# Another issue order for the backward chain of a memory-augmented attention kernel

## The chip, the cores and the metric

The kernel runs on one core of a Trainium2 chip. The metric is the device time of one execution in microseconds (us); the time before is the median of three runs, 2872.61 us (2855.53 to 2875.89). The engines are TensorE (PE; its weight loads are shown as PEld), VectorE (DVE), ScalarE (ACT), GpSimd (POOL) and SyncE (SP), which issues DMAs. GpSimd issues DMAs too.

## The reference

The reference computes a forward pass and all its gradients. The forward is a residual sum of two branches over the same normalised rows: an attention branch that walks over 64 segments of 32 rows and carries 8 memory rows from one segment to the next, and a dense branch with a squared relu.

```python
def _A_ref(x, mem0, Wq, Wk, Wv, Wo, seg_len):
    ...
    for s in range(n_seg):
        xs = x[:, s * seg_len:(s + 1) * seg_len, :].copy()
        h = jnp.concatenate([mem, xs], axis=1)
        q = jnp.einsum('btd,dhe->bhte', h, Wq)
        k = jnp.einsum('btd,dhe->bhte', h, Wk)
        v = jnp.einsum('btd,dhe->bhte', h, Wv)
        scores = jnp.einsum('bhqe,bhke->bhqk', q, k) * scale
        scores = jnp.where(mask[None, None], scores, -1000000000.0)
        p = _softmax(scores, axis=-1)
        o = jnp.einsum('bhqk,bhke->bhqe', p, v)
        o = jnp.einsum('bhte,hed->btd', o, Wo)
        mem = o[:, :M, :].copy()
        outs.append(o[:, M:, :])
    return jnp.concatenate(outs, axis=1)
...
    xn = _layernorm(x, axis=-1)
    return x + _A_ref(xn, A_mem0, A_Wq, A_Wk, A_Wv, A_Wo, A_seg_len) + _B_ref(xn, B_w1, B_b1, B_w2, B_b2)
...
_out, _vjp = jax.vjp(_f, A_x, A_mem0, A_Wq, A_Wk, A_Wv, A_Wo, B_w1, B_b1, B_w2, B_b2)
_grads = _vjp(grad_out)
```

There are 2048 rows of 512, 32 heads of 128. In the backward pass the gradient of a segment's memory rows is what the segment before it needs, so the 64 segments are a chain, walked from the last to the first.

## The kernel before

The kernel runs in stages: the dense branch, the forward chain, a stage for the left parts' softmax gradients with the dense weights' gradients beside it, the backward chain (from 1348.5 us of the profiled span to about 2310), and the large weight gradients at the end. This change is in the backward chain alone.

A *step* of the chain is one segment; four steps are a *block*. I number the steps in the order in which the chain walks them, so that steps 20 to 23 are the first to fourth step of one block. A step has some 60 small operations, each a function that issues a handful of instructions, and an operation has a name:

- o0mm, o1mm (L374): the incoming gradient times Wo, 16 matmuls each; o0ev, o1ev copy the result to SBUF (gON); o0fl, o1fl (L167) transpose it and o0te, o1te copy that (gOT);
- vp0, vp1 (L1389, L1391): products with the probabilities, PD, which pb (L1337) builds on GpSimd out of the loaded P; vea, veb, vla, vlb copy them out into gv and gvL;
- s0, s1 (L464): products with the values, vT, which vc (L1351, L1352) builds on GpSimd out of vl, loaded by vtr (L1346, a transposing DMA); d10 to d41 and tu0, tu1 are the softmax gradient on VectorE;
- kp0, kp1 and qp0, qp1 (L623): gradients of keys and queries, 32 small matmuls each; kea0 to keb1, kla0 to klb1, qea0 to qeb1 copy them out of PSUM into gk, gkL and gq, on ScalarE (L419) or VectorE (L422);
- vg0 to qg1 (L492): "gathers", gv, gk and gq times the weights, 16 matmuls each, summed in ps_gR; the sixth is done in two halves;
- ra, rb, ta, tb, Ha, Hb, xa, xb: the sum R is copied, transposed (L528) and added over head groups; Ha and Hb write the memory rows' gradient into GT, from which the next step's o0mm starts.

An operation that begins with L. is one of the block's "left" part, done once a block for the block before or beside it: L.G0 to L.I3 (L1256) are 12 groups of 8 matmuls, L.ta, L.tb their transposes, L.Vo, L.Ko, L.Qo (L1243) the stores of the block's gv, gk, gq (the tile G4, one buffer) to DRAM, L.sx (L1291) the store of XT, L.ldv and L.ldk loads for the next block. ldp, ldq, ldn (L1332, L1339, L1340) load the next step's P, qN and kN on GpSimd's queue.

The order is written out by hand, in B_ORDER: four strings, one for each step of a block. The number of plus signs behind a name says by how many rounds or steps it is shifted, so that a string may hold operations of several steps. Each engine, and each engine's DMA queue, runs its operations strictly in that order. ENGS says which copies run on ScalarE and which on VectorE.

TensorE's matmuls come in three tile forms, as the profile's rows show them: 128*32 (o0mm, s0, the gathers, L.G to L.I), 32*128 (kp, qp) and 128*128 (o0fl, vp, the transposes). TensorE's order in the four steps of a block, before:

```
1: o0mm o1mm o0fl vp0 L.G2 s0 o1fl vp1 L.I1 L.G1 s1 kp0 vg1 qp0 vg0 kg0 qp1 qg0 kp1 qg1 kg1 L.H2 ta tb
2: o0mm o1mm o0fl vp0 s0 o1fl vp1 L.H1 s1 vg0 kp0 qp0 vg1 qg0 kp1 kg0 qp1 L.I2 kg1 qg1 L.G3 ta tb
3: o0mm o1mm o0fl vp0 s0 o1fl vp1 vg0 s1 kp0 vg1 qp0 L.I3 kg0 kp1 qp1 qg0 kg1 qg1 L.H3 ta tb
4: o0mm o1mm o0fl vp0 o1fl s0 vp1 s1 vg0 L.G0 kp0 L.tb qp0 vg1 kg0 kp1 qp1 L.ta qg0 kg1 qg1 L.I0 ta tb L.H0
```

Of the kernel before, what the change touches and what calls it, by code (L numbers as in the profile page):

```python
# [26 lines left out]
def kernel(  # L27
# [673 lines left out]
    with psum("fr", 4) as fr, psum("fpp", 1) as fpp, \  # L701
# [259 lines left out]
        with tc.manual_schedule():  # L961
# [25 lines left out]
            for n in range(-1, NB + 4):  # L987
                play(F_ORDER, n, steps, lefts, lambda s: s, lambda b: b, done)
# [5 lines left out]
    with sb("la", 2) as la, sb("ls", 2) as ls, sb("lo", 1) as lo_, sb("wg", 2) as wg, psum("lpp", 1) as lpp, psum("lr", 4) as lr:  # L994
# [170 lines left out]
        "pb+++ rb+++ ldq+++ L.H2+ ta+++ tb+++ vc+++ Ha+++ Hb+++ o0mm++++ o0ev++++ o1mm++++ o1ev++++ xb+++ o0fl++++ "  # L1165
# [20 lines left out]
    with sb("bq", 1) as bq, sb("bt", 1) as bt, sb("bs", 2) as bs, sb("be", 1) as be, psum("bpp", 1) as bpp, psum("br", 4) as br:  # L1186
# [274 lines left out]
        with tc.manual_schedule():  # L1461
# [225 lines left out]
```

## Time and profile before

| | us |
|---|---|
| three runs | 2855.53, 2872.61, 2875.89 |
| span of the profiled execution | 2875.6 |
| backward chain, first to last step's start | 1348.5 to 2281.2 |
| TensorE busy in it | 849.3 |
| steps 20, 21, 22, 23 | 16.55, 13.05, 13.45, 15.45 |

The profile gives no time of its own beside the span; the slowest of the three runs is 0.3 us above it. In a row of instructions stand the line, engine, operation, what it writes <- what it reads, the tile form and sizes, the count, the busy time and the mean of one in ns, and then the idle time before them with what ended it. In a table of windows each column is an engine's busy time with the count of its instructions, then the granted TensorE clock, the share of time in which the DMA engines were busy, and GB/s. "Issue" is waiting that the profile explains by no semaphore.

### The profile page before, as it was taken

The numbers are of one execution on the slowest core, as the hardware profiler recorded it, in microseconds if no ns is written. First come the engines' busy times: TensorE is split into PE (matmuls) and PEld (weight loads), VectorE is DVE, ScalarE is ACT, GpSimd is POOL, SyncE is SP. The second block draws the span as 40 slices with busy tenths as digits, with TensorE's granted clock in tenths as the row PEclk, the third lists the DMA queues.
The fourth block names the chain that finished last, engine by engine and source line by source line (L and its number), as shares of the span: only waits on it lengthen the run. The fifth ranks groups of instructions, "written<-read, shape, count | busy, mean of one in ns | idle before, by whom it ended". The sixth has DMA issues, their size and how long they took to land.

```text
span 2875.6 us, 116922 instructions
## 1 busy us (share of the span) xinstructions
PE 2672.8 (93%) x52315; PEld 1447.4 (50%) x52405; DVE 1277.0 (44%) x3755; ACT 1001.7 (35%) x2330; POOL 665.8 (23%) x1289
## 2 busy tenths in 40 slices
PE   7998999999999997788898989999999899999999
PEld 3444555555555555355444544554445444444444
DVE  4534656666666655343444544554445401100000
ACT  2324544444444445232333333333334311111111
POOL 1000000000000000223333433343333434322221
PEclk9999999999999999899999999999999999999999
DMA  9865689899999888987577876788777899999993
GB/s 248 268 204 172 157 201 222 204 215 225 211 208 226 205 210 186 283 243 205 140 172 168 192 210 168 171 195 213 175 168 183 224 294 271 216 211 209 211 207 69
DMA packets 839066, 586.77 MB, mean 204 GB/s; under 512 B 638001, under 2 KB 727618, under 8 KB 835234
## 3 DMA queue, kind: packets, MB, share of 16 engines
q1 hardware_dynamic: 796034, 450.52, 69.2%
q0 software_dynamic: 42384, 128.63, 15.2%
q8 instruction: 411, 6.73, 1.0%
q14 instruction: 93, 0.76, 0.1%
q10 hardware_dynamic: 144, 0.13, 0.0%
HBM read 184.95 MB, written 248.79 MB: 151 GB/s over the span
## 4 chain that ended last, share of the span: by engine, by line
PE 84%; DMA 6%; issue 4%; DVE 4%; ACT 1%; SPq 1%; POOL 0%; ACTq 0%; DVEq 0%; POOLq 0%
PE ps_gw L1645 19%; PE ps_proj L374 16%; PE ps_gR L492 11%; PE ps_R L492 5%; PE ps_tr L167 3%; PE ps_L L374 3%; PE b_pp L623 3%; PE ps_RL L1256 2%; PE ps_sc L464 2%; PE f_pp L623 2%; PE ps_w L1106 2%; PE ps_h L310 2%; PE ps_B L345 2%; PE ps_gxb L354 2%; PE ps_ga L317 2%
## 5 line engine op out<-in xcount | busy, mean ns | idle before, releaser
L1645 PE MATMUL ps_gw<-gn,HNc 128*128 128x512 bf16 x1884 | 414.6, 379 | 1.9
L1645 PEld LDWEIGHTS <-HNc 128*128 128x128 bf16 x1920 | 187.9, 98 | 223.8
L419 ACT CAST f_N<-ps_proj 128x512 bf16<-128x512 f32 x320 | 184.0, 581 | 196.0 <-PE ps_proj L374 189.3
L1579 ACT CAST wt<-ps_gw 128x512 bf16<-128x512 f32 x128 | 73.5, 589 | 437.8 <-PE ps_gw L1645 404.9
L374 PEld LDWEIGHTS <-X 128*32 128x32 bf16 x5760 | 144.8, 96 | 136.0 <-DVE X L537 20.2
L884 POOL COPY kM<-f_kT 128x256 bf16<-128x256 bf16 x64 | 25.8, 403 | 756.3 <-DVE f_kT L422 571.6
L1562 DVE TENSOR_TENSOR gx<-ps_rows,gb 128x512 f32<-128x512 f32 x16 | 11.1, 692 | 402.1 <-PE ps_rows L1560 402.1
L492 PE MATMUL ps_gR<-Wv,gv 128*32 128x512 bf16 x2048 | 143.0, 397 | 8.3 <-issue 8.3
L492 PE MATMUL ps_gR<-Wk,gk 128*32 128x512 bf16 (+1 forms) x2048 | 141.6, 386 | 4.2 <-issue 3.6
L492 PE MATMUL ps_R<-Wo,OT 128*32 128x256 bf16 x4096 | 131.8, 279 | 11.9 <-issue 6.3
L1645 PE MATMUL ps_gw<-GOc,gn 128*128 128x512 bf16 x626 | 138.4, 379 | 2.0 <-DMA GOc<-in_grad_out_dram 1.3
L492 PE MATMUL ps_gR<-Wq,gq 128*32 128x512 bf16 (+1 forms) x2048 | 127.1, 359 | 8.0 <-issue 7.9
L419 ACT CAST gON<-ps_proj 128x512 bf16<-128x512 f32 x128 | 75.0, 586 | 160.2 <-PE ps_proj L374 160.2
L374 PE MATMUL ps_proj<-Wq,X 128*32 128x512 bf16 x1920 | 127.3, 380 | 1.9 <-issue 1.9
L374 PE MATMUL ps_proj<-Wo,GT 128*32 128x512 bf16 x2048 | 123.8, 384 | 5.4 <-DVE GT L1301 5.0
L1580 POOL DMA_DIRECT2D out_dram<-wt x120 | 65.0, 544 | 262.0 <-ACT wt L1579 239.8
L374 PE MATMUL ps_proj<-Wk,X 128*32 128x512 bf16 x1920 | 124.6, 382 | 1.0 <-issue 0.2
L374 PE MATMUL ps_proj<-Wv,X 128*32 128x512 bf16 x1920 | 121.9, 378 | 0.0
L419 ACT CAST gk<-b_pp 128x256 bf16<-128x256 f32 x192 | 69.2, 379 | 146.4 <-PE b_pp L623 104.8
L1332 POOL DMA_DIRECT2D b_P<-S_A x63 | 33.9, 538 | 369.2 <-issue 128.4
L1337 POOL COPY PD<-b_P 32x320 bf16<-32x320 bf16 x256 | 115.6, 451 | 8.9 <-DMA b_P<-S_A 0.3
L492 PEld LDWEIGHTS <-OT 128*32 128x32 bf16 x4096 | 105.7, 98 | 21.0 <-issue 14.1
(291 smaller groups left out, 5280.6 us busy)
## 6 DMA issues: line engine op xcount, KB each, us to landing
S_A<-f_N SPq DMA_DIRECT2D x64, 512.0 KB
out_dram<-wt POOLq DMA_DIRECT2D x134, 128.0 KB, 5.4
S_A<-f_N SPq DMA_DIRECT2D x64, 256.0 KB
S_GB<-gv SPq DMA_DIRECT2D x32, 512.0 KB
S_GB<-gk SPq DMA_DIRECT2D x32, 512.0 KB
S_GB<-gq SPq DMA_DIRECT2D x32, 512.0 KB
b_kN<-S_A POOLq DMA_DIRECT2D x63, 256.0 KB, 4.4
b_qN<-S_A POOLq DMA_DIRECT2D x63, 256.0 KB, 4.3
```

Source lines behind the costliest of these rows:

```text
L167: nc.tensor.transpose(ps_ap, in_ap, ident[base:base + k, base:base + k])
L310: nc.tensor.matmul(ps[:], lhsT=W1[:, dc, fc * P:(fc + 1) * P], rhs=HT[:, dc, :], start=(dc == 0), stop=(dc == DC - 1))
L317: nc.tensor.matmul(ps2[:], lhsT=W2T[:, dc, fc * P:(fc + 1) * P], rhs=gT[:, dc, :], start=(dc == 0), stop=(dc == DC - 1))
L345: nc.tensor.matmul(psB[:], lhsT=aT[:, fc, rc * P:(rc + 1) * P], rhs=W2[:, fc, :], start=(fc == 0), stop=(fc == FC - 1))
L374: nc.tensor.matmul(o, lhsT=hT[:, dc, :], rhs=x, start=(dc == 0), stop=(dc == DC - 1), tile_position=(0, 32 * g))
L419: nc.scalar.copy(out, in_)
L492: nc.tensor.matmul(R[32 * g:32 * g + 32, 0:(cs.stop - cs.start) * P].rearrange("p (a b) -> p a b", b=P), lhsT=XT(k, g), rhs=x[:, cs, :], s ...
L623: nc.tensor.matmul(o, lhsT=N_[32 * g:32 * g + m, kk * P:(kk + 1) * P], rhs=X(kk)[32 * g:32 * g + m], start=(i == 0), stop=(i == len(jobs) ...
L1337: nc.gpsimd.tensor_copy(PD[32 * g:32 * g + 32, g], C["P"][32 * g:32 * g + 32, :, KW - L:KW])
L1579: nc.scalar.copy(wt[:], ps[:])
L1580: eng(dst, wt[:])
L1645: nc.tensor.matmul(ps[:], lhsT=l(rc), rhs=r(rc), start=(n == 0), stop=(n == RC_ALL - 1))
```

## The change

B_ORDER is written anew, with the same operations. Its four strings are cut at another place (a string begins in the middle of one step and ends in the middle of the next), which is why the loops begin at -2. Three copies of a step go from ScalarE to VectorE (kea0, kla1, qea1) and two from VectorE to ScalarE (klb0, qeb1). TensorE's order in the four steps of a block, after:

```
1: o0mm o1mm L.H0 o0fl vp0 o1fl s0 vp1 s1 L.I1 L.G1 vg1 kp0 qp0 vg0 kg0 kp1 qp1 qg0 qg1 kg1 L.H2 ta tb
2: o0mm o1mm o0fl vp0 s0 L.H1 vp1 o1fl vg0 s1 kp0 qp0 vg1 L.I2 qg0 kp1 qp1 kg0 kg1 qg1 ta tb
3: o0mm o1mm o0fl vp0 o1fl s0 vp1 L.G3 L.I3 s1 kp0 qp0 vg0 vg1 kg0 qp1 kp1 qg0 kg1 qg1 L.H3 ta tb
4: o0mm o1mm o0fl vp0 s0 vp1 o1fl L.ta L.tb s1 vg0 kp0 qp0 vg1 kg0 kp1 qp1 L.G0 qg0 L.I0 kg1 qg1 L.G2 ta tb
```

The loads and stores move too. Where a fourth step meets the next first one, SyncE's queue was L.Vo0 L.Vo1 L.qtr L.Ko0 L.lq L.Ko1 L.qst ldk0 ldk1 L.Qo0 | L.Qo1 L.sx vtr, and is L.qtr L.ldt L.lq L.qst L.Vo1 | L.Ko0 L.Vo0 L.Qo1 ldk0 L.Qo0 ldk1 L.sx L.Ko1 vtr (the bar is the step's start in the written order). GpSimd's queue was vc L.ldv L.ldk | pb ldn ldp ldq ldp ldn pb ldq vc, and is L.ldv pb L.ldk ldq vc | ldn ldp ldq ldp ldn vc pb.

```diff
--- before.py
+++ after.py
@@ -984,7 +984,7 @@
                     for i in range(m):
                         ps = fr.tile([P, 8 * P], BF16, name="ps_wt", tag="r")
                         turn_weight(ps, *q.pop(0), acp if k in ("L.S1", "L.ex0", "L.ex1") else (acp, vcp)[i % 2])
-            for n in range(-1, NB + 4):
+            for n in range(-2, NB + 4):
                 play(F_ORDER, n, steps, lefts, lambda s: s, lambda b: b, done)
     sm_cm.__exit__(None, None, None)
     assert not TURNS_O
@@ -1156,33 +1156,37 @@
 
 
     B_ORDER = (
-        "L.vo0+ o0mm++++ o1mm++++ L.vo1+ L.Qo1+ o0ev++++ pb+++ xa+++ L.xt o1ev++++ o0fl++++ xb+++ L.ra0+ vp0++++ "
-        "o0te++++ L.G2+ vea++++ s0++++ d10++++ o1fl++++ d20++++ L.ko0+ d30++++ vla++++ o1te++++ vp1++++ "
-        "ldn+++ L.I1+ L.G1+ d40++++ ldp++++ ldq+++ veb++++ s1++++ d11++++ vlb++++ kp0++++ ldp+++++ vg1++++ L.qo0+ "
-        "tu0++++ L.qo1+ keb0++++ d21++++ qp0++++ kla0++++ L.sx+ vg0++++ kea0++++ d31++++ qeb0++++ d41++++ vtr++++ "
-        "L.ko1+ kg0++++ klb0++++ tu1++++ qp1++++ ldn++++ qeb1++++ qea0++++ qg0++++ qea1++++ kp1++++ qg1++++ keb1++++ "
-        "kea1++++ kg1++++ klb1++++ kla1++++ ra++++",
-        "pb+++ rb+++ ldq+++ L.H2+ ta+++ tb+++ vc+++ Ha+++ Hb+++ o0mm++++ o0ev++++ o1mm++++ o1ev++++ xb+++ o0fl++++ "
-        "vp0++++ xa+++ o0te++++ vla++++ s0++++ o1fl++++ vp1++++ d10++++ vea++++ vtr++++ d20++++ L.H1+ o1te++++ L.ktr+ "
-        "d30++++ d40++++ veb++++ vlb++++ tu0++++ vtr+++++ s1++++ d11++++ d21++++ ldp+++++ d31++++ vg0++++ kp0++++ "
-        "qp0++++ d41++++ vg1++++ qea0++++ qeb0++++ qg0++++ keb0++++ L.kst+ tu1++++ kla0++++ klb0++++ kp1++++ kea0++++ "
-        "kea1++++ kg0++++ qp1++++ keb1++++ kla1++++ qeb1++++ L.ra1+ L.I2+ kg1++++ qea1++++ L.ra2+ qg1++++ klb1++++ "
-        "ra++++ L.G3+ rb++++ ta++++ Ha++++",
-        "vc+++ tb+++ Hb+++ ldq+++ o0mm++++ xb+++ o1mm++++ o0ev++++ o0fl++++ pb+++ xa+++ o1ev++++ o0te++++ vp0++++ "
-        "s0++++ d10++++ vea++++ d20++++ o1fl++++ L.vtr+ vp1++++ o1te++++ vg0++++ vla++++ s1++++ d30++++ d40++++ "
-        "d11++++ L.sl ldn+++ veb++++ tu0++++ d21++++ vlb++++ kp0++++ keb0++++ vg1++++ d31++++ d41++++ L.vst+ L.gs+ "
-        "kea0++++ qp0++++ tu1++++ qea0++++ klb0++++ kla0++++ L.I3+ kg0++++ qeb0++++ kp1++++ L.gl++ qp1++++ ldp+++++ "
-        "qea1++++ kea1++++ keb1++++ qeb1++++ qg0++++ klb1++++ kla1++++ L.gst+ kg1++++ ldq++++ qg1++++ ra++++ L.H3+ "
-        "ta++++ rb++++ Ha++++ tb++++ Hb++++",
-        "o0mm++++ o1mm++++ o0ev++++ vc+++ L.ra3+ ldn+++ xb+++ vtr++++ o1ev++++ xa+++ L.ldt++ o0fl++++ pb+++ vp0++++ "
-        "vc++++ o1fl++++ o0te++++ s0++++ vea++++ vla++++ o1te++++ d10++++ d20++++ vp1++++ s1++++ d30++++ veb++++ "
-        "vlb++++ d40++++ d11++++ vg0++++ L.G0++ kp0++++ L.Vo0++ L.Vo1++ L.tb+ kla0++++ tu0++++ d21++++ qp0++++ vg1++++ d31++++ keb0++++ "
-        "d41++++ kea0++++ kg0++++ kp1++++ L.qtr+ qeb0++++ tu1++++ klb0++++ qp1++++ L.ldv++ L.ta+ qea0++++ "
-        "qg0++++ qeb1++++ kea1++++ L.Ko0++ keb1++++ qea1++++ kg1++++ L.lq++ klb1++++ qg1++++ L.I0++ ra++++ L.ldk++ L.Ko1++ rb++++ "
-        "ta++++ L.qst+ ldk0++++ ldk1++++ L.Qo0++ kla1++++ tb++++ L.H0++ Ha++++ Hb++++")
+        "d20+++++ d30+++++ vg0+++++ d40+++++ vla+++++ o1te+++++ tu0+++++ s1+++++ vtr++++++ kp0+++++ veb+++++ "
+        "vlb+++++ qp0+++++ d11+++++ d21+++++ vg1+++++ qeb0+++++ L.I2+ d31+++++ qea0+++++ qg0+++++ d41+++++ tu1+++++ "
+        "kp1+++++ keb0+++++ qp1+++++ vc+++++ kea0+++++ kla0+++++ kea1+++++ qea1+++++ klb0+++++ keb1+++++ pb+++++ "
+        "L.ko1+ kg0+++++ ldq+++++ L.vo0+ ldn+++++ qeb1+++++ kg1+++++ qg1+++++ L.vtr+ klb1+++++ ra+++++ vc++++++ "
+        "kla1+++++ rb+++++ ta+++++ L.gst+ L.vst+ Ha+++++ tb+++++ L.ko0+ Hb+++++ o0mm++++++ xa+++++ L.gl++ xb+++++ "
+        "o1mm++++++ o0ev++++++ o0fl++++++ o1ev++++++ vp0++++++ vtr+++++++ o1fl++++++ L.ra1+ o0te++++++ s0++++++ "
+        "vp1++++++ o1te++++++ vla++++++ d10++++++ d20++++++",
+        "d30+++++ d40+++++ tu0+++++ L.G3+ L.I3+ s1+++++ kp0+++++ qp0+++++ d11+++++ vea+++++ d21+++++ vg0+++++ "
+        "vlb+++++ d31+++++ veb+++++ vg1+++++ kea0+++++ d41+++++ klb0+++++ L.sl tu1+++++ keb0+++++ kg0+++++ L.vo1+ "
+        "qp1+++++ L.qtr+ qea0+++++ ldp++++++ kp1+++++ kea1+++++ qeb0+++++ qea1+++++ pb+++++ kla0+++++ keb1+++++ "
+        "qg0+++++ qeb1+++++ L.ra2+ kla1+++++ kg1+++++ qg1+++++ ra+++++ klb1+++++ L.H3+ ta+++++ rb+++++ tb+++++ "
+        "Ha+++++ Hb+++++ xb+++++ o0mm++++++ L.ra3+ o1mm++++++ o0ev++++++ o0fl++++++ vp0++++++ o1ev++++++ xa+++++ "
+        "vea++++++ o0te++++++ s0++++++ L.ldt++ vp1++++++ d10++++++ o1fl++++++ L.ta+ L.tb+ d20++++++ vla++++++ "
+        "ldq+++++ o1te++++++ d30++++++ ldn+++++ s1++++++",
+        "d40+++++ tu0+++++ vg0+++++ veb+++++ L.lq++ vlb+++++ kp0+++++ qp0+++++ d11+++++ d21+++++ d31+++++ L.ldv++ "
+        "vg1+++++ kea0+++++ keb0+++++ pb+++++ kg0+++++ d41+++++ kp1+++++ tu1+++++ qeb0+++++ qea0+++++ klb0+++++ "
+        "L.qst+ qp1+++++ kla0+++++ kla1+++++ L.ldk++ kea1+++++ keb1+++++ qeb1+++++ L.G0++ L.xt+ qg0+++++ L.I0++ "
+        "kg1+++++ L.Vo1++ klb1+++++ qea1+++++ qg1+++++ L.G2++ ra+++++ rb+++++ ta+++++ tb+++++ Ha+++++ ldq+++++ "
+        "Hb+++++ vc+++++ o0mm++++++ o0ev++++++ o1mm++++++ L.H0++ ldn+++++ L.Ko0++ L.Vo0++ xa+++++ o0fl++++++ "
+        "o1ev++++++ vp0++++++ o0te++++++ L.qo1++ xb+++++ L.Qo1++ ldk0+++++ o1fl++++++ ldp+++++++ s0++++++ vp1++++++ "
+        "o1te++++++ L.Qo0++ d10++++++ d20++++++ s1++++++",
+        "L.ra0++ ldk1++++ L.sx++ d30+++++ d40+++++ tu0+++++ L.Ko1++ vla+++++ L.I1++ veb+++++ d11+++++ L.G1++ "
+        "vg1+++++ L.qo0 kp0+++++ vlb+++++ qp0+++++ d21+++++ vea+++++ ldq+++++ keb0+++++ kea0+++++ vtr+++++ d31+++++ "
+        "vg0+++++ d41+++++ qeb0+++++ kg0+++++ vtr++++++ L.ktr++ kla0+++++ tu1+++++ klb0+++++ kp1+++++ qp1+++++ "
+        "qea1+++++ ldp+++++ qea0+++++ qeb1+++++ qg0+++++ keb1+++++ ldn+++++ qg1+++++ klb1+++++ kea1+++++ vc+++++ "
+        "kg1+++++ ra+++++ L.H2++ kla1+++++ ta+++++ rb+++++ tb+++++ L.gs++ Ha+++++ L.kst++ Hb+++++ xb+++++ xa+++++ "
+        "pb+++++ o0mm++++++ o0ev++++++ o1mm++++++ o0fl++++++ vp0++++++ o0te++++++ o1ev++++++ vea++++++ s0++++++ "
+        "ldp+++++++ d10++++++ L.H1++ vp1++++++ o1fl++++++")
     ENGS = on_engines(
-        "L.ra0 kea0 keb0 keb1 kla0 kla1 o0ev o1ev qea0 qea1 qeb0 ra vea veb vla vlb",
-        "kea1 klb0 klb1 o0te o1te qeb1")
+        "L.ra0 keb0 keb1 kla0 klb0 o0ev o1ev qea0 qeb0 qeb1 ra vea veb vla vlb",
+        "kea0 kea1 kla1 klb1 o0te o1te qea1")
     with sb("bq", 1) as bq, sb("bt", 1) as bt, sb("bs", 2) as bs, sb("be", 1) as be, psum("bpp", 1) as bpp, psum("br", 4) as br:
         G4 = {n: bq.tile([P, HG, KH, SPB, SEG], BF16, name="g" + n) for n in "vkq"}
         gS = bq.tile([P, KH, KW], BF16, name="gS")
@@ -1484,7 +1488,7 @@
                     steps[NSEG - s][n] = steps[NSEG - 1 - s][n]
             for n in ("vtr", "vc", "ldp", "pb", "ldq", "ldn", "ldk0", "ldk1"):
                 steps[0][n] = lambda: None
-            for n in range(-1, NB + 4):
+            for n in range(-2, NB + 4):
                 play(B_ORDER, n, steps, lefts, lambda s: NSEG - 1 - s, lambda b: NB - 1 - b)
 
             ps = big("ps_m0")
```

## The prediction

> **What bounds the kernel now.** I read the page first, for the busy shares and the chain that ended last.
>
> ```profile
> span 2875.6 us, 116922 instructions
> ...
> PE 2672.8 (93%) x52315; PEld 1447.4 (50%) x52405; DVE 1277.0 (44%) x3755; ACT 1001.7 (35%) x2330; POOL 665.8 (23%) x1289
> ...
> q8 instruction: 411, 6.73, 1.0%
> ...
> PE 84%; DMA 6%; issue 4%; DVE 4%; ACT 1%; SPq 1%; POOL 0%; ACTq 0%; DVEq 0%; POOLq 0%
> ```
>
> TensorE carries 84% of the chain, so what TensorE does not have to do, or does not have to wait for, comes off the end. Next the windows: the whole backward chain, then four successive steps of one block of it (steps 20 to 23, called first to fourth below), then two stretches that I use later.
>
> ```profile
> core 0: us, PE busy (x) PEld busy (x) DVE busy (x) ACT busy (x) POOL busy (x), PEclk, DMA share, GB/s
> 1709.00:1721.27 12.27, 10.26 (x253) 5.99 (x254) 5.67 (x20) 4.15 (x10) 2.73 (x6) 1.00 1.15 377
> ...
> 1761.34:1767.47 6.13, 3.27 (x127) 1.74 (x127) 1.00 (x4) 1.41 (x5) 4.17 (x10) 1.00 1.19 164
> ...
> 1348.50:2281.20 932.70, 849.30 (x22416) 463.05 (x22416) 453.68 (x1420) 354.60 (x960) 357.57 (x694) 0.97 0.74 180
> 1654.00:1670.55 16.55, 13.61 (x368) 7.14 (x356) 6.87 (x25) 6.12 (x16) 4.87 (x10) 1.00 0.94 269
> 1670.55:1683.60 13.05, 12.90 (x356) 7.24 (x356) 7.89 (x23) 5.35 (x15) 4.68 (x9) 1.00 0.53 119
> 1683.60:1697.05 13.45, 12.52 (x349) 6.94 (x348) 6.33 (x21) 5.63 (x15) 2.45 (x5) 1.00 0.43 110
> 1697.05:1712.50 15.45, 14.01 (x361) 7.79 (x364) 8.26 (x24) 5.50 (x15) 10.66 (x22) 1.00 0.99 239
> ```
>
> The chain's 932.7 us hold 849.3 us of busy TensorE: 83.4 us of waiting. The middle steps take 13.05 and 13.45 us, the first 16.55 and the fourth 15.45, and those two are the ones with a DMA share near 1. Then the waits of TensorE within the chain say for whom it waited.
>
> ```profile
> PE b_pp L623 <- issue: 28.5, 23, 3.2
> PE ps_gR L492 <- issue: 19.8, 17, 3.8
> PE b_pp L623 <- DMA b_qN<-S_A: 8.5, 4, 3.8
> PE ps_proj L374 <- DVE GT L1301: 5.0, 1, 5.0
> PE ps_sum L545 <- issue: 4.0, 1, 4.0
> PE b_pp L623 <- DMA b_qNL<-S_NL: 2.9, 1, 2.9
> ```
>
> Three rows of "issue" make 28.5 + 19.8 + 4.0 = 52.3 us, most of the 83.4. "Issue" is a wait that no semaphore explains. I read it as late instructions: queue q8 moved 6.73 MB in 411 packets, and 6.73 MB over 52315 + 52405 instructions of TensorE is 64 bytes each, so a packet holds about 255 of them. Two stretches that I cut from the end of one issue wait to the end of a later one hold 253 + 254 = 507 and 127 + 127 = 254 matmuls and weight loads: two packets and one. TensorE stops where a packet ends, when DMA is busy (shares 1.15 and 1.19).
>
> **The change part by part.** *Fewer changes of tiling.* I sort TensorE's operations by the tile form in their rows (128*32, 32*128, 128*128) and count the neighbours of different form in the two written orders: 51 in a block of four steps before, 40 after (14, 12, 12, 13 against 10 each); over the chain, edges included, 814 and 641. The price is in start-to-start times:
>
> ```profile
> 1675.96 0.20 PE L623 MATMUL b_pp<-gS,b_qN 32*128 32x40 bf16 x4
> ...
> 1676.17 0.21 PE L623 MATMUL b_pp<-gST,b_kN 32*128 32x32 bf16 x4
> ...
> 1676.55 1.05 PE L492 MATMUL ps_gR<-Wv,gv 128*32 128x512 bf16 x16
> 1677.42 1.04 PE L492 MATMUL ps_gR<-Wq,gq 128*32 128x512 bf16 x16
> 1678.39 0.20 PE L623 MATMUL b_pp<-gS,b_qN 32*128 32x40 bf16 x4
> ```
>
> ```profile
> 1660.29 0.20 PE L623 MATMUL b_pp<-gS,b_qN 32*128 32x40 bf16 x4 [1.35 <-DVE ds_t L579]
> ...
> 1660.58 1.05 PE L492 MATMUL ps_gR<-Wv,gv 128*32 128x512 bf16 x16
> ```
>
> A kp followed by a qp of its own form takes 1676.17 - 1675.96 = 0.21 us, one followed by a gather 1660.58 - 1660.29 = 0.29. A gather followed by a gather takes 1677.42 - 1676.55 = 0.87, one followed by a kp 1678.39 - 1677.42 = 0.97. So a change costs 0.08 to 0.10 us, and 173 fewer are worth 173 x 0.09 = **-15.6 us** (13.8 to 17.3), all on TensorE. The Trainium skill ("TensorEngine Tiling (Array Packing)", Key Properties) says that a change of tiling mode drains the engine, and its page "TensorE: Matmul & The Clock Gate" (Step-by-step: what each phase is for) puts the drain near 128 cycles of a 2.4 GHz clock, which as an estimate is 0.053 us, or 9 us for 173. The rows show more, and I take the rows.
>
> *Loads moved.* Behind the two L.ldk loads of the fourth step the old GpSimd queue has pb (four PD copies), then the loads of kN and P, then that of qN for the first step; the new one has pb ahead of L.ldk and qN right behind it. In the old first step qN can land as late as kp0 needs it. The new place gives it the four copies (0.451 us each, row below) and two issues more. I take most of the 8.5 us of waits for b_qN: **-8** (0 to -11.4, with b_qNL).
>
> *Stores moved.* The next rows are the chain in the first step, and SyncE's issues just before.
>
> ```profile
> 1655.07 8.45 DMA S_GB<-gq
> 1663.59 0.38 ACT gq L419
> 1664.22 0.36 DVE gST L482
> 1664.72 0.37 PE b_pp L623 x32
> ```
>
> ```profile
> 1652.64 0.54 SPq L1243 DMA_DIRECT2D S_GB<-gk  x1
> ...
> 1655.07 1.79 SPq L1243 DMA_DIRECT2D S_GB<-gq  x2
> 1656.95 1.26 SPq L1291 DMA_DIRECT2D S_XG<-b_XT  x1
> 1658.46 4.04 SPq L1346 DMA_TRANSPOSE b_vl<-S_A  x1
> ```
>
> ```profile
> 1664.72 0.20 PE L623 MATMUL b_pp<-gST,b_kN 32*128 32x32 bf16 x4 [0.55 <-DVE gST L482]
> ```
>
> G4 has one buffer, so the first copy into gq waits until the store of the last block's gq has read it, 8.45 us after issue; behind it VectorE's transpose, and behind that qp1, 0.55 us late. The new queue puts both gq stores ahead of L.sx and of the second gk store (L.Ko1), and I reckon them out some 3 us earlier: **-8** for 16 blocks x 0.5 (0 to -16). The price is that L.Ko1 comes last, behind L.sx, which waits for xb of the next step: out about 4.5 us into the step instead of 1.4 before its start (1652.64 against 1654.00). With 8.45 us to read, keb1 and kea1 may write at 13, where the stall-free order wants them at about 9 (the starts above, added up to kp1 and qp1) and a step of 16.55 at 12 or later.
>
> *Also in that step*, GpSimd does vc (1.041 + 0.413) before pb (4 x 0.451 = 1.8), where it did pb first:
>
> ```profile
> L1337 POOL COPY PD<-b_P 32x320 bf16<-32x320 bf16 x256 | 115.6, 451 | 8.9 <-DMA b_P<-S_A 0.3
> L1351 POOL COPY b_vT<-b_vl 128x1024 bf16<-128x1024 bf16 x64 | 66.6, 1041 | 70.9 <-DMA b_vl<-S_A 40.0 <-PE ps_sc L464 29.5
> ...
> L1352 POOL COPY b_vT<-b_vTL 128x256 bf16<-128x256 bf16 x64 | 26.4, 413 | 4.2 <-DMA b_vTL<-S_NL 4.1
> ```
>
> The vl transpose goes out behind L.Ko1, at about 5.5; landing like the store before it, 8.5 later, at 14. Then vc to 15.5, pb to 17.3, and vp0 of the next step, 2.1 us into it, needs that pb: the first step cannot be under 15.2 us. It took 16.55 here, so this holds a further gain back rather than adding. For both together I take **+5** (0.3 a block; 0 to 3.5 a block is 0 to +56, the rival below).
>
> *Instruction packets.* kp and qp are 32 matmuls and 32 weight loads in 0.21 to 0.30 us, by far the densest work. Old first step, kp0 to kp1: 4 x 64 + 4 x 32 = 384 instructions in 0.29+0.98+0.30+0.87+0.97+0.30+0.97+0.29 = 4.97 us, 3.3 us a packet. New: kp0 qp0 vg0 kg0 kp1 qp1, 4 x 64 + 2 x 32 = 320 in 0.21+0.30+0.87+0.97+0.21+0.30 = 2.86 us, 2.3 us a packet. A packet in time for 3.3 us can be 1 us late for 2.3; there is one such stretch in each of the two DMA-heavy steps, so 0 to 32 x 1 = +32. The neighbouring packets get thinner, and most give it back: I take a quarter, **+8**. The Trainium skill ("Runtime: NRT & Kernel Launch", Instruction fetch mechanics) says instructions come in blocks of 256 and that fetching is hidden behind the issue of the block before. The 256 agrees with 507 and 254 here; the hiding does not, at 52.3 us of issue waits.
>
> *A filler is gone.* After the last gather R is copied out before ta can start:
>
> ```profile
> L419 ACT COPY R<-ps_gR 128x512 f32<-128x512 f32 x63 | 37.0, 587 | 93.7 <-PE ps_gR L492 93.7
> ```
>
> In the old order eight matmuls of the block's left part (0.53 us) stand there in every step; in the new second step none does. Of the 0.587 some 0.2 is exposed already, so 0.3 more: 16 x 0.3 = **+5** (0 to 9).
>
> *Copies moved.* A step takes from ScalarE two copies of 128x256 and one of 128x64 and gives it one of each: one 128x256 net, to VectorE. VectorE is busy 453.7 of 932.7 us and ScalarE 354.6, so about 0.4 us a step hides in VectorE's idle half: **0**. Uncovered it would be 64 x 0.4 = 26 us. The forward loop's start at -2 adds an empty round: 0.
>
> Sum: -15.6 - 8 - 8 + 5 + 8 + 5 = **-13.6 us**. The profiled span is 2875.6, 3 us over the median of the runs shown (2872.6); taken off the median, 2859.
>
> **The rivals.** *The first step opens up.* If the loads, the stores and the issue waits of the first step unwind together, it falls from 16.55 towards the bound of 15.2 worked out above: 1.35 x 16 = 22 us, with the switches and the filler -22 - 15.6 + 5 = -32, 2840. For it: the granted clock averages 0.97 over the chain, so fewer gaps may also bring clock back, at most 0.03 x 933 = 28 us. Against: the DMA share there stays near 1.
>
> *Nothing arrives.* First and fourth step are held by DMA and instruction packets, not by TensorE's work; the 11 changes saved in a block are half in these steps, so only -7 remains, and the filler takes 5: 2870.
>
> *Slower: the late gk store.* keb1 and kea1 wait for L.Ko1, kg1 waits for them, and pb for the late vl. It decides from the point where L.Ko1 goes out more than 4.5 us into the step or takes more than 8.5 us to read. At 3.5 us a block it is +56 for the +5: 2859 + 51 = 2910.
>
> *Instructions are always in time.* By the skill's rule the +8 is nothing and the issue waits are something else: 2851. The 507 and 254 speak against it.
>
> **How the numbers follow.** About 1%, 29 us, is what a measurement of this kernel tells from no change, given runs from 2855.5 to 2875.9. Forecast (2845 to 2867, the fourth rival in it): 0.38, of which 0.05 the rival's. Nothing arrives (2867 to 2890): 0.18. First step opens (2810 to 2848): 0.24. Slower by the store (2885 to 2930): 0.20. Forecast at **2859**. The range 2822 to 2905 leaves out about a tenth at each end. Below 2844 lies most of the opening case, 0.23; above 2901 most of the slower one, 0.17, and I add 0.03 for waits that I have not seen; the rest, 0.57, is within 1%.
>
> **What the changed profile would show.** A kp followed by its qp at 0.21 us wherever they are neighbours, and TensorE's busy time in the chain lower by up to 15. No wait on b_qN. ScalarE waiting for the gk store instead of the gq store. "Issue" rows of 50 to 65 us, concentrated on L623 and L492. Second step near 12.7 to 13 us with a wait before b_T, third near 13. First step 15.5 to 16.5; if it is over 18, the store rival is true. Wrong would be the whole working if the middle steps grew: then a wait stands in an order that I took for clear.

## The result, and the profile after

The changed kernel is slower by 0.4%: 2883.09 us, median of 20 runs (2866.45 to 2902.82), against 2868.99 us for 20 runs of the kernel before (2855.53 to 2884.90). The ratio is 1.0042, with a 95% interval of 1.0024 to 1.0060. The forecast was 2859, with a gain as its likeliest sign. The profiled execution after took 2873.27 us, its span is 2871.3. It lies 10 us under its kernel's median and the profiled execution before (2875.89) 7 us over its own, so the totals of these two profiles have the other sign than the medians; what I read in them is the stages.

First the page after: the span, the busy times, the queue of the instructions, and the shares of the chain that ended last.

```profile
span 2871.3 us, 116970 instructions
...
PE 2657.6 (93%) x52405; PEld 1451.7 (51%) x52405; DVE 1295.2 (45%) x3819; ACT 975.2 (34%) x2266; POOL 663.4 (23%) x1289
...
q8 instruction: 411, 6.73, 1.0%
...
PE 82%; DMA 7%; issue 4%; DVE 4%; ACT 2%; SPq 1%; POOL 0%; ACTq 0%; DVEq 0%; POOLq 0%
```

On this page nearly nothing has moved: TensorE has 82% of the chain instead of 84%. The averages hide two stages that went opposite ways. The windows show them: after, the backward chain from first to last step's start, then the final stage (the large weight gradients, from the first matmul of ps_gw to the end), then steps 20 to 23; in the second fence the final stage before, which starts at 2312. The columns are those of the prediction's tables.

```profile
1340.30:2244.10 903.80, 823.33 (x22412) 466.07 (x22412) 471.79 (x1483) 329.50 (x897) 356.56 (x694) 0.98 0.77 186
2273.00:2871.30 598.30, 567.17 (x2624) 259.87 (x2623) 56.02 (x96) 79.31 (x160) 171.43 (x276) 0.97 1.03 195
1627.50:1646.45 18.95, 14.90 (x366) 8.18 (x366) 7.00 (x22) 5.56 (x15) 4.89 (x10) 0.91 0.79 191
1646.45:1659.21 12.76, 12.20 (x349) 7.01 (x348) 6.93 (x22) 5.16 (x14) 4.65 (x9) 1.00 0.46 99
1659.21:1672.65 13.44, 12.81 (x358) 7.36 (x358) 7.97 (x24) 5.16 (x14) 4.35 (x9) 1.00 0.83 162
1672.65:1686.95 14.30, 13.40 (x361) 7.72 (x360) 8.26 (x27) 5.07 (x14) 8.75 (x17) 1.00 0.84 268
```

```profile
2312.00:2875.60 563.60, 557.21 (x2574) 257.93 (x2624) 56.03 (x96) 79.72 (x160) 169.54 (x272) 1.00 1.02 208
```

The chain is 28.9 us shorter in this execution (932.7 to 903.8), with 26.0 us less of busy TensorE. The final stage, in which no operation was changed, is 34.7 us longer (563.6 to 598.3), at the same share of DMA and a granted clock of 0.97 instead of 1.00: 10.0 us of it are more busy TensorE (567.2 against 557.2), the other 24.7 are waiting. (Step 20 is an unlucky first step, with its clock at 0.91; over steps 8 to 59 the first steps take 15.99 us on average, where they took 17.22.)

Why the final stage grew is in its waits of TensorE. The first fence is from after, the second from before.

```profile
PE ps_gw L1649 <- DMA GOc<-S_GM: 13.1, 1, 13.1
PE ps_rows L1564 <- ACT wt L1583: 11.2, 1, 11.2
PE ps_gw L1649 <- ACT wt L1583: 3.2, 1, 3.2
```

```profile
PE ps_gw L1645 <- DMA GOc<-in_grad_out_dram: 1.3, 1, 1.3
```

Now follow the missing GOc back. This is GpSimd's timeline after, then the piece of the chain that ended last just ahead of it, then the two issues on SyncE's queue that it names.

```profile
2259.18 0.52 POOL L1602 DMA_DIRECT2D GOc<-in_grad_out_dram  x1 [1.10 <-DMA gn<-S_ON]
2277.14 2.21 POOL L1537 DMA_DIRECT2D gn<-S_OL  x4 [17.44 <-DMA S_GB<-gv]
2279.34 1.51 POOL L1527 DMA_DIRECT2D gn<-S_ON  x2
...
2288.84 0.56 POOL L1598 DMA_DIRECT2D GOc<-S_GM  x1 [1.56 <-DMA gn<-S_OL]
```

```profile
2269.17 1.18 SPq L1275
2270.39 6.12 DMA S_GB<-gv
2276.58 0.55 issue
2277.14 1.38 POOL gn L1537 x3
```

```profile
2265.82 0.71 SPq L1247 DMA_DIRECT2D S_GB<-gv  x1
...
2270.39 1.04 SPq L1247 DMA_DIRECT2D S_GB<-gv  x1
```

GpSimd waits 17.44 us in front of one load. load_left(0) writes a tile that, as the releaser in its row says, lies where gv lay in the chain, so it may start only when the last block's gv has been stored. In the kernel before, the same load has no such wait:

```profile
2303.42 0.58 POOL L1533 DMA_DIRECT2D gn<-S_OL  x1 [1.42 <-ACT b_R L419]
```

The store of gv has two halves, L.vo0 and L.vo1, issued only for the last block. The old order has both early (they go out at 2285.54, 4 us after the last step's start); the new strings have L.vo1 nearly at the very end, at 2270.39. Behind the waiting load stand the second column's loads and GOc's first row, which goes out at 2288.84 and is what TensorE waits for from about 2307 on. The Trainium skill ("DMA: Bandwidth & Descriptors", Anatomy of one DMA — SWDGE (gpsimd) path) says that DMA engines do not wait on semaphores, but the issuing sequencer does before it dispatches. The 17.44 us are that wait, on the one sequencer that issues all the rest.

SyncE's queue shows a second side of it, after and then before:

```profile
2278.67 45.38 SPq L1620 DMA_TRANSPOSE HNc<-S_HT  x2
```

```profile
2344.01 8.60 SPq L1616 DMA_TRANSPOSE HNc<-S_HT  x1
```

The transposing loads of HNc start 5.6 us into the final stage instead of 32.0, because the stores that they stand behind on SyncE's queue have landed sooner (3.5 us of waiting for those, against 17.5 before), and all four take 82.9 us instead of 31.3. They run beside GpSimd's late loads. GOc's row takes 31.7 us to land, where in e1 below it takes 18.4; with 18.4 it would have been there at 2307.2, just as TensorE needs it. No run moved these transposes alone, so their part of the cost is argued from the traces, not shown.

### The profile page after: what moved, and what is told of

Same layout as the page of the kernel before. It is cut to its first block, busy times and chain, and to the rows that moved or that the text cites. A ratio compares the mean times of both kernels' runs of the same rounds, so it can differ in the third digit from the quotient of the medians.

```text
span 2871.3 us, 116970 instructions
## 1 busy us (share of the span) xinstructions
PE 2657.6 (93%) x52405; PEld 1451.7 (51%) x52405; DVE 1295.2 (45%) x3819; ACT 975.2 (34%) x2266; POOL 663.4 (23%) x1289
## 3 DMA queue, kind: packets, MB, share of 16 engines
q0 software_dynamic: 42384, 128.63, 15.6%
q8 instruction: 411, 6.73, 1.0%
## 4 chain that ended last, share of the span: by engine, by line
PE 82%; DMA 7%; issue 4%; DVE 4%; ACT 2%; SPq 1%; POOL 0%; ACTq 0%; DVEq 0%; POOLq 0%
PE ps_proj L374 16%; PE ps_gw L1649 16%; PE ps_gR L492 12%; PE ps_R L492 5%; PE ps_tr L167 3%; PE ps_RL L1260 3%; PE ps_L L374 3%; PE b_pp L623 3%; DMA gn<-S_ON 2%; PE ps_sc L464 2%; PE f_pp L623 2%; PE ps_w L1111 2%; PE ps_B L345 2%; PE ps_w L1106 2%; PE ps_gxb L354 2%
## 5 line engine op out<-in xcount | busy, mean ns | idle before, releaser
L1566 DVE TENSOR_TENSOR gx<-ps_rows,gb 128x512 f32<-128x512 f32 x16 | 11.1, 691 | 379.3 <-PE ps_rows L1564 379.3
L1649 PE MATMUL ps_gw<-GOc,gn 128*128 128x512 bf16 x640 | 145.8, 391 | 17.4 <-DMA GOc<-S_GM 13.1
L492 PE MATMUL ps_gR<-Wv,gv 128*32 128x512 bf16 x2048 | 135.9, 389 | 7.7 <-issue 5.7
L492 PE MATMUL ps_gR<-Wk,gk 128*32 128x512 bf16 (+1 forms) x2048 | 130.7, 378 | 5.1 <-issue 5.0
L492 PE MATMUL ps_gR<-Wq,gq 128*32 128x512 bf16 (+1 forms) x2048 | 118.6, 351 | 6.4 <-issue 6.4
L1341 POOL COPY PD<-b_P 32x320 bf16<-32x320 bf16 x256 | 114.8, 448 | 16.1 <-DMA b_P<-S_A 4.0
L1649 PEld LDWEIGHTS <-gn 128*128 128x128 bf16 x640 | 64.4, 101 | 97.2 <-issue 26.4
L492 PEld LDWEIGHTS <-gq 128*32 128x32 bf16 x2816 | 74.5, 98 | 54.9 <-issue 18.8
```

The lines of the kernel that those rows point to most:

```text
L492: nc.tensor.matmul(R[32 * g:32 * g + 32, 0:(cs.stop - cs.start) * P].rearrange("p (a b) -> p a b", b=P), lhsT=XT(k, g), rhs=x[:, cs, :], s ...
L1341: nc.gpsimd.tensor_copy(PD[32 * g:32 * g + 32, g], C["P"][32 * g:32 * g + 32, :, KW - L:KW])
L1649: nc.tensor.matmul(ps[:], lhsT=l(rc), rhs=r(rc), start=(n == 0), stop=(n == RC_ALL - 1))
```

## The experiments

Twelve runs were made, each of one kernel beside the kernel before on the same chip; a second execution of the changed kernel and one of e11 (e12, e13) are among them. All but e3 have the chain's new order. "e1" in the column of edits means the changed kernel with e1's edit. The ratio is an estimate from the runs of both kernels on one chip and not the plain quotient of the medians (for e1 that would be 2852.13 / 2871.97 = 0.9931). The diffs of the order show only the pieces of its strings that change.

| run | edit | median us (runs) | ratio to before, 95% |
|---|---|---|---|
| after | the change | 2883.09 (20) | 1.0042 (1.0024 to 1.0060) |
| e1_gv_first | gv stores of the last block early | 2852.13 (12) | 0.9951 (0.9923 to 0.9979) |
| e2_all_six | all six of its stores early | 2853.64 (12) | 0.9940 (0.9912 to 0.9968) |
| e3_before_late | before, six stores late | 2898.03 (7) | 1.0089 (1.0050 to 1.0128) |
| e11_left_later | after, load_left(0) later | 2870.46 (12) | 1.0004 (0.9976 to 1.0032) |
| e5_apart | e1, kp0 and qp0 apart | 2854.87 (11) | 0.9929 (0.9896 to 0.9961) |
| e6_loads | e1, loads put back | 2846.00 (6) | 0.9904 (0.9870 to 0.9938) |
| e7_filler | e1, L.I2 last | 2850.47 (6) | 0.9899 (0.9864 to 0.9935) |
| e8_store | e1, L.Ko1 ahead of L.sx | 2854.07 (12) | 0.9941 (0.9913 to 0.9969) |
| e9_best | e1, e6 and e7 together | 2843.24 (8) | 0.9904 (0.9871 to 0.9938) |
| e10_less_dma | e1, 90 of 96 stores left out | 2804.29 (4) | 0.9767 (0.9719 to 0.9815) |

### The store of gv, taken out of the way and put in the way

```diff
-L.ko1+ kg0+++++ ldq+++++ L.vo0+ ldn+++++
+L.ko1+ kg0+++++ ldq+++++ ldn+++++
-keb0+++++ kg0+++++ L.vo1+
+keb0+++++ kg0+++++
-Hb+++++ vc+++++ o0mm++++++
+Hb+++++ L.vo0++ L.vo1++ vc+++++ o0mm++++++
```

> The changed kernel with one thing moved: the two stores of the last block's gv, L.vo0 and L.vo1, go out right after Hb of the last step, where the kernel before has them; the other four stores of that block stay late. Theory A (GpSimd's queue is blocked): load_left(0) writes into the place where gv was, waits for the late L.vo1, and holds up every load of the final stage queued behind it. Then the chain stays at about 931 us from the first o0mm to its end, the wait of about 17 us before the loads of S_OL goes, the three waits of TensorE in the final stage (13.1, 11.2, 3.2 us) go, the final stage falls from 599.8 us to 565 to 572, and the time from 2883 to 2850 to 2858, ratio to the kernel before 0.993 to 0.996. Theory B (the final stage is late because the chain ends earlier and the DMA engines are full, share 1.0 to 1.3 either way): the stage stays at 590 to 600 us and the time at 2875 to 2885.

The time falls to 2852.13. Its windows (chain, final stage), and SyncE's and GpSimd's rows for the same store and load:

```profile
1342.00:2245.70 903.70, 825.28 (x22412) 467.36 (x22412) 472.27 (x1483) 329.54 (x897) 356.33 (x694) 0.98 0.77 186
2275.70:2840.90 565.20, 558.73 (x2574) 258.29 (x2623) 56.04 (x96) 80.09 (x160) 167.73 (x270) 1.00 1.01 206
```

```profile
2249.92 0.84 SPq L1247 DMA_DIRECT2D S_GB<-gv  x2
```

```profile
2265.95 0.57 POOL L1537 DMA_DIRECT2D gn<-S_OL  x1 [1.02 <-DMA GOc<-S_GM]
```

The store goes out 20 us earlier, the load no longer waits for it (the 1.02 us are for another transfer), the final stage is back at 565.2 us with the clock at 1.00, and the chain is what it was. Theory A holds: the late store of gv is what lengthens the final stage. Next, beside e1's edit, the other four stores:

```diff
-"L.ko1+ kg0+++++
+"kg0+++++
...
-tb+++++ L.ko0+ Hb+++++
+tb+++++ Hb+++++
...
-L.qo1++ xb+++++
+xb+++++
...
-"L.ra0++ ldk1++++ L.sx++ d30+++++
+"L.ra0++ L.ko0++ L.qo0++ L.qo1++ ldk1++++ L.sx++ L.ko1++ d30+++++
...
-L.qo0 kp0+++++
+kp0+++++
```

> The changed kernel with all six stores of the last block (gv, gk, gq, two each) back at the places relative to the left part's groups that they had before. Theory A (only the store of gv is in the way): the same as with gv's stores alone, within 5 us. If the gk and gq stores hold something too, another 3 to 10 us less. Theory B (full DMA engines): 2875 to 2885, as with gv alone.

2853.64, and a final stage of 566.4 us: the other four add nothing. The reverse, in the kernel before:

```diff
-"L.vo0+ o0mm++++ o1mm++++ L.vo1+ L.Qo1+ o0ev++++ pb+++ xa+++ L.xt
+"o0mm++++ o1mm++++ L.Qo1+ o0ev++++ pb+++ xa+++ L.qo1+ L.xt
-d20++++ L.ko0+ d30++++
+d20++++ d30++++
-vg1++++ L.qo0+ "
-"tu0++++ L.qo1+ keb0++++
+vg1++++ "
+"tu0++++ keb0++++
-"L.ko1+ kg0++++
+"kg0++++
...
-L.ra1+ L.I2+ kg1++++
+L.ra1+ L.I2+ L.ko1+ L.vo0+ kg1++++
...
-L.sl ldn+++
+L.sl L.qo0 ldn+++
...
-Ha++++ tb++++ Hb++++",
+Ha++++ tb++++ Hb++++ L.ko0+ L.vo1+",
```

> The kernel before with nothing changed but the six stores of the last block, put in the order of the changed kernel (gv's second half and gq's first half last). Theory A: the chain as before (962 us), the final stage 20 to 35 us longer (585 to 600 instead of 565), the time 2889 to 2904, ratio 1.007 to 1.012. Theory B: nothing moves, 2865 to 2873.

2898.03, 26 us (0.89%) over before. The final stage grows by 20 us, with the same two waits as in the changed kernel, on the old chain. The windows (chain, final stage), TensorE's waits, and GpSimd's wait in front of load_left(0):

```profile
1350.80:2283.10 932.30, 852.89 (x22412) 465.48 (x22412) 452.48 (x1420) 354.32 (x960) 357.08 (x694) 0.97 0.74 180
2312.60:2896.20 583.60, 559.94 (x2574) 258.45 (x2624) 56.04 (x96) 79.31 (x160) 171.41 (x276) 0.99 1.03 201
```

```profile
PE ps_gw L1645 <- DMA GOc<-S_GM: 13.9, 1, 13.9
PE ps_rows L1560 <- ACT wt L1579: 3.5, 1, 3.5
```

```profile
2320.89 2.21 POOL L1533 DMA_DIRECT2D gn<-S_OL  x4 [19.91 <-DMA out_dram<-gm]
```

The profile puts the end of this wait down to the store of gm, which went out at 2316.84, 3 us behind gv's second half (2313.64). The load doesn't need that one: in the kernel before it goes out at 2303.42, and the store of gm only at 2326.05. Here too the transposes of HNc start early (10.1 us into the stage) and GOc's row takes 30.5 us to land.

So the late stores cost 26 us on the old chain, and the late store of gv costs about as much on the new one (1.0042 - 0.9951 = 0.0091 of 2870 is 26; by the medians, each against its own runs of before, 34). It needs no other part of the change.

### Is it the store, or what is queued behind the load?

```diff
-        load_left(0, pdma)
         got[1] = columns(1)
         ...
         go_rows(0, pdma)
+        load_left(0, pdma)
         loads(2)
```

> The changed kernel with all its stores where the change put them; in the final stage alone, load_left(0), the four loads that write where gv was, is issued behind the loads of the second column and GOc's first row instead of ahead of them. Theory A (not the store's lateness itself, but the loads queued behind the waiting load_left(0) cost the time): the wait of 13.1 us for GOc in the final stage goes or falls under 3, the stage falls from 598 us to 565 to 575, and the time from 2883 to 2850 to 2862. Rival (TensorE needs the rows of load_left(0) themselves, and they are late): TensorE waits for gn<-S_OL instead, the stage stays at 585 to 600, the time at 2870 to 2885.

2870.46 is 13 us below the changed kernel and 18 above e1: both theories have a part. The profiled execution was the fastest of twelve (2859.28), with a final stage of 569.6 us, so a second one was taken.

> The kernel with load_left(0) behind the second column's loads once more, for a second profiled execution: the first one was the fastest of twelve (2859 against a median of 2870). If the part that this edit does not give back (some 15 us of 28 in the medians) is the rows of load_left(0) themselves coming late in slower executions, TensorE's wait for gn<-S_OL is 5 to 20 us here instead of 1.7, and the final stage 575 to 590 us. Rival: the stage is again 568 to 572 and the slower executions lose their time in the chain, 915 to 930 us between first and last step.

It took 2866.09 us. TensorE's waits for loads in the final stage, first execution and then second:

```profile
PE ps_gw L1649 <- DMA gn<-S_GL: 2.8, 3, 1.3
PE ps_gw L1649 <- DMA gn<-S_OL: 1.7, 1, 1.7
```

```profile
PE ps_gw L1649 <- DMA gn<-S_OL: 13.5, 1, 13.5
```

With the queue freed, the wait for GOc is gone, and the rows of load_left(0) themselves become what is late, in the second execution by 13.5 us (final stage 580.4 us). By the medians the queue is some 40% of the cost (13 of 31 us); that the rest is the late data of load_left(0) rests on this one execution.

> The changed kernel itself, for a second profiled execution: the first one took 2873 us, 10 under the median of 20. If the executions differ in the chain, its first to last step takes 910 to 920 us instead of 904 with the final stage again at 595 to 600; if they differ in the final stage, that is 605 to 615 us with waits for GOc over 15 us. Either way the wait for GOc<-S_GM is over 10 us and the chain under 920 us, against 932.3 and 932.7 in the two executions with the order before.

The changed kernel's second execution took 2888.72 us (one run of the kernel before beside it 2887.68): chain 917.7, final stage 585.4. TensorE's two waits in it, and GpSimd's row:

```profile
PE ps_rows L1564 <- ACT wt L1583: 12.0, 1, 12.0
PE ps_gw L1649 <- DMA GOc<-S_GM: 4.7, 1, 4.7
```

```profile
2303.61 2.21 POOL L1537 DMA_DIRECT2D gn<-S_OL  x4 [16.97 <-DMA S_GB<-gv]
```

That the wait for GOc would be over 10 us again, and the final stage at least as long, was wrong. GpSimd's wait for the store of gv is the same (16.97 after 17.44), and GOc's row goes out as late (16.1 us into the stage after 15.8), but here it lands in 21.5 us instead of 31.7. What the wait turns into further on differs between executions.

### The terms of the chain

In each step qp0 is put one gather later; the second step as an example:

```diff
-kp0+++++ veb+++++ vlb+++++ qp0+++++ d11+++++ d21+++++ vg1+++++ qeb0+++++
+kp0+++++ veb+++++ vlb+++++ d11+++++ d21+++++ vg1+++++ qp0+++++ qeb0+++++
```

> The changed kernel with the two gv stores early, and in each step qp0 put one gather later, so that a gather stands between kp0 and qp0: 769 changes of the tiling in the chain instead of 641, 128 more. If a change costs 0.08 to 0.10 us, TensorE's busy time in the chain rises by 10 to 13 us over the 825 and 830 us of the two runs with that order, while thinner instruction packets give back up to 8 us of the issue waits (57 and 64 us there): the time is 2853 to 2866 against 2852. Rival: the changes cost nothing at the end, and the gain of the chain came from the loads and stores: busy time and chain as in those two runs (904 and 917 us), the time 2848 to 2856.

The time does not move: 2854.87 lies in both ranges. The starts in step 21 show why, of e1 (kp0, qp0, vg1, L.I2) and then of this kernel (kp0, vg1, qp0, L.I2):

```profile
1654.22 0.20 PE L623 MATMUL b_pp<-gS,b_qN 32*128 32x40 bf16 x4
...
1654.43 0.21 PE L623 MATMUL b_pp<-gST,b_kN 32*128 32x32 bf16 x4
...
1654.81 1.05 PE L492 MATMUL ps_gR<-Wv,gv 128*32 128x512 bf16 x16
1655.68 0.60 PE L1260 MATMUL ps_RL<-Wq,b_gqL 128*32 128x512 bf16 x8
```

```profile
1653.05 0.20 PE L623 MATMUL b_pp<-gS,b_qN 32*128 32x40 bf16 x4
...
1653.34 1.05 PE L492 MATMUL ps_gR<-Wv,gv 128*32 128x512 bf16 x16
1654.32 0.19 PE L623 MATMUL b_pp<-gST,b_kN 32*128 32x32 bf16 x4
...
1654.62 0.61 PE L1260 MATMUL ps_RL<-Wq,b_gqL 128*32 128x512 bf16 x8
```

The same three operations take 1655.68 - 1654.22 = 1.46 us with two changes and 1654.62 - 1653.05 = 1.57 with four: 0.055 a change (the medians over 15 blocks are 1.46 and 1.57 too). This is a net price: a kp with a qp right behind it does take 0.21, but then the qp takes 0.38, where it takes 0.30 alone. The prediction's own rows hold that 0.38 (1676.55 - 1676.17), and I read only the row ahead of it. Beside this, thinner packets gave back: the rows of "issue" in the chain add up to 45.8 us, against 56.9 and 64.2 in e1 and e2, while 13.6 us of waits for the copies of gk and gq (8.5 and 5.1) are new.

```profile
PE ps_gR L492 <- DVE gk L422: 8.5, 15, 0.6
...
PE ps_gR L492 <- ACT gq L419: 5.1, 16, 0.8
```

Next, each by itself on e1, the loads, the filler and the store (e6, e7 and e8):

```diff
-keb0+++++ pb+++++ kg0+++++
+keb0+++++ kg0+++++
-L.ldk++ kea1+++++
+L.ldk++ pb+++++ kea1+++++
-Ha+++++ ldq+++++ "
+Ha+++++ "
-L.H0++ ldn+++++ L.Ko0++
+L.H0++ ldn+++++ ldq+++++ L.Ko0++
```

> The changed kernel with the two gv stores early, and GpSimd's queue put back: the copies of P (pb) of the fourth step behind L.ldk instead of ahead of it, and the load of qN behind that of kN. If the place of these loads was worth the 8 us of the prediction, waits of TensorE for b_qN and b_qNL come back at 4 to 11 us, nearly all in the first step, and the time is 2856 to 2863 against 2852. Rival: the load of qN lands in time either way in this order, since kp0 comes no earlier: no such waits, the time 2848 to 2856.

```diff
-qeb0+++++ L.I2+ d31+++++
+qeb0+++++ d31+++++
-qg1+++++ L.vtr+ klb1+++++
+qg1+++++ L.I2+ L.vtr+ klb1+++++
```

> The changed kernel with the two gv stores early, and L.I2 of the second step put behind the last gather, where the copy of R is waited for. If the missing filler costs the 5 us of the prediction, the waits of TensorE for ScalarE's R ahead of b_T (5.1 us in 17 waits) go to under 1, and the time is 2846 to 2849 against 2852. Rival: L.I2 covered as much where it stood (ahead of qg0, which needs qp0's copies), so the wait only moves to qg0: the waits for R go, waits or busy time ahead of qg0 come, the time stays within 2 us.

```diff
-L.sx++ d30+++++ d40+++++ tu0+++++ L.Ko1++ vla+++++
+L.Ko1++ L.sx++ d30+++++ d40+++++ tu0+++++ vla+++++
```

> The changed kernel with the two gv stores early, and the second gk store of each block (L.Ko1) ahead of L.sx instead of behind it on SyncE's queue. If the late store costs the 5 us of the prediction (keb1 and kea1 late in the first step), the first step falls by about 0.3 us a block and the time to 2845 to 2849 against 2852. Rival: the store is read in time where it is (no wait of ScalarE or VectorE for S_GB in the traces of this order), so nothing moves, 2849 to 2856.

e6: the wait for qN comes back, as expected, at 4.6 us in 5 waits, yet the time is 2846.00, not higher. Its issue rows add up to 51.4 us, 5.5 under e1. e7: the waits ahead of b_T fall from 5.1 us to 0.9, and the time (2850.47) lies within e1's spread. e8: nothing moves (2854.07). The intervals of these three overlap e1's, so no difference from e1 is shown for any of them. e6 speaks against the loss of 4 to 11 us that the term of the loads would have brought back; whether e6 and e7 gain something over e1 (6 and 2 us by the medians, 13 and 15 by the ratios) isn't settled. The rows are e6's wait for qN and then e1's for R, which e7 removes.

```profile
PE b_pp L623 <- DMA b_qN<-S_A: 4.6, 5, 2.0
```

```profile
PE b_T L528 <- ACT R L419: 5.1, 17, 0.3
```

> The changed kernel with the two gv stores early, pb of the fourth step behind L.ldk, the load of qN behind that of kN, and L.I2 behind the last gather: the three edits that did no harm alone, together. If the loads' edit gives its 6 us and the filler's its 2 us (medians of 2846 and 2850 against 2852 with the stores alone), the time is 2842 to 2848, ratio 0.987 to 0.991. Rival: both differences were the spread of the runs, and the time is 2849 to 2856.

2843.24 us, as expected, against 2874.47 for the kernel before in the same runs: the fastest version with the whole work, 1.0% faster than before and 1.4% than the change (0.9904 / 1.0042 = 0.986). Whether the two edits beside e1's add to it isn't settled, since its interval overlaps e1's.

### What the issue waits are

```diff
-                        dma(S_GB[b, t][:, gs, ks], ...)
+                        if b == 0:
+                            dma(S_GB[b, t][:, gs, ks], ...)
...
-                                                S_GB[4 * q + x, t][:, g]...
+                                                S_GB[0, t][:, g]...
```

> The changed kernel with the two gv stores early, and without the stores of gv, gk and gq of the first 15 blocks (48 MB less to DRAM in the chain); the final stage reads the last block's rows in their place, so the gradients of the weights are not the reference's. If the issue waits are instruction packets that come late because the DMA engines are full, they fall from 57 to 64 us to under 30, the DMA share of the chain from 0.77 to under 0.5, the first step from 15.4 to 16.1 us to under 14.5, and the time to 2800 to 2830. Rival (the issue waits have another cause, in TensorE's own queue): they stay over 50 us, and the time falls by less than 10 us.

The chain's window and then the two largest issue rows of its waits:

```profile
1349.40:2209.50 860.10, 814.21 (x22412) 463.49 (x22412) 472.85 (x1483) 329.28 (x897) 357.86 (x694) 0.99 0.62 140
```

```profile
PE b_pp L623 <- issue: 17.4, 28, 1.9
...
PE ps_gR L492 <- issue: 2.6, 5, 0.8
```

TensorE runs the same instructions (411 packets, 6.73 MB on q8 here too). Without the stores the issue rows fall from 56.9 us (e1) to 22.4, the first step from 15.38 to 13.24 us, the time to 2804.29; the chain is 43.6 us shorter, of which 11.1 are less busy TensorE. Only the DMA share (0.62) misses the expectation. The traces tie these waits to the packets, each of which has 16 KB: of the 44 issue waits over 0.3 us in e1's chain, 42 end 1.2 to 1.7 us after a packet of q8 has landed (31 of 31 in this run), and a moment picked at random lies in that distance in one case of ten. So most of the issue waits are instruction packets that come late behind the kernel's own stores. The Trainium skill ("Runtime: NRT & Kernel Launch", Instruction fetch mechanics) says that the issue of instructions hides their fetching; 57 us against 22 us, with nothing but stores left out, say that in this kernel it doesn't always.

## Why the prediction was wrong

**The step that failed** is the one that ends the sum: the six terms are all in the chain's steps, and their sum was "taken off the median", so the final stage was held unchanged. The part *Stores moved* looked at the stores of the blocks walked over (L.Ko, L.Qo) and not at the six lower-case stores of the last block, which the diff moves too and which have their own places in the strings. The missing term is +26 us. The rival "slower: the late gk store" had the right kind of cause, a store that comes too late for what overwrites it, at the wrong place; with L.Ko1 put early (e8) nothing moves. The measured 2883 us lies in the interval of the rival "nothing arrives" (2867 to 2890), but not for its reason: the chain did gain.

**The sum of the chain was about right.** With the store out of the way, e1, e2 and e8 are 14 to 17 us faster than before (0.9951, 0.9940, 0.9941), against the -13.6 forecast. With the +26 that e3 measures by itself, that makes +9 to +12, against the measured +12. In the profiles the chain's gain looks larger, 22 us: 932.7 and 932.3 us in two executions of the old order, 903.7 to 917.7 in six of the new one (910 on average). Single executions of one order differ by 14 us, so the first pair of profiles, with 28.9, overstated it.

That the sum came out is in part luck. In the same two and six executions the 16 first steps together are 23.7 us shorter (279.5 to 255.8), and the other steps together 1.1 us longer, although TensorE is 10.0 us less busy in them. So the changes of tiling saved there (7 of the 11 of a block, not half, as the rival "nothing arrives" has it) don't show in their time, and the gain came where the rival "the first step opens up" looked for it, at about the 22 us that it gave for that step. The third step, which the prediction wanted near 13, grew from 13.04 to 13.33 us (steps 8 to 59), but L.G3 was moved into it from the second (13.15 to 13.05).

Term by term, from these two and six executions (waits summed over the rows of the view, in the chain):

- *Changes of tiling*, -15.6: the count stands, the price of 0.09 doesn't. At 0.055 (e5, which puts 128 changes of the same kind back) 173 are worth 10 us, as an estimate. The estimate from the Trainium skill ("TensorE: Matmul & The Clock Gate", Step-by-step: what each phase is for), 0.053 and 9 us, which I set aside for the rows, is near this number; whether the drain is its cause isn't shown, since 0.055 is a net price.
- *Loads moved*, -8: the waits for loads go from 13.9 and 8.2 us to 0.8 or less, so the wait was read rightly; but e6 brings half of it back at no cost in time.
- *Stores moved*, -8: ScalarE's wait for the gq store (3.8 us before) is gone, the wait for the gk store that was expected in its place doesn't come, and the first step falls from 17.22 and 16.77 to 15.86 us. Its parts can't be told apart. *The late L.Ko1 and vc before pb*, +5: e8 shows no difference for the store; the bound of 15.2 us for the first step was wrong, since 5 of the 16 first steps in the profiled execution of the changed kernel are under it (the shortest 14.3).
- *Instruction packets*, +8: issue waits of 51.7 and 54.6 us before, 57 to 64.5 after, 61 on average. The term and its size held: the thinner packets of e5 have 45.8, and e10 shows what makes them late.
- *Filler gone*, +5: 1.0 to 1.8 us before, 5.1 to 5.4 after. Held.
- *Copies moved*, 0: in the chain ScalarE is 25 us less busy and VectorE 18 more, and no wait of TensorE names them. The copies' assignment alone wasn't tried, since the order's engines wait for one another by it.

What no term held is the clock. TensorE is 24 us less busy in the chain (851 to 827 on average), of which 10 are changes of tiling by the estimate above; in the record of the granted clock the stretches at 0.5 within the chain are 15 and 16 in the old order and 9 to 12 in the new one, 14 us of lost clock less on average. The rival "the first step opens up" had this at "at most 28". Why there are fewer stretches is open; no run changed that alone.

## What to carry to other kernels

When an order is rewritten, go through what is issued once (first and last block) as carefully as the loop: here a gain of 14 to 17 us went under in one store put last. Look up what reuses the memory that a moved store reads; a load that waits for it holds up everything behind it on its queue, in the next stage too. And when pricing an edit from neighbouring rows, measure from the start of the group to the start of what follows the whole group, not to the next row.

## What the runs showed beside that

TensorE's instructions compete with the kernel's own DMA: leaving out 90 stores of 0.5 MB took 35 us of issue waits off a chain of 904 us and all of what made the first step some 2.3 us longer than the middle ones. Stores spread over the four steps might be worth more in this chain than the orders of TensorE's work tried here; that wasn't tried. Another surprise is how a wait of 17 us on one queue costs the final stage 20 to 35 us. A second wait, of 3.5 to 12 us (ps_rows on wt), follows the first: in the changed kernel's trace the chain that ended last leads there through GpSimd's queue, where the first store of the output (out_dram<-wt, at 2343.93) goes out after 22.40 us of waiting for loads of gn<-S_ON, and ScalarE's copies and TensorE wait in turn for these stores.
